# Three tiles of scans a batch instead of four, the fourth head pair joined by transfers, and state products in four tiles of TensorE

## The chip, the cores and the metric

One Trainium2 chip, one of its cores. TensorE (PE, with its weight loads PEld), VectorE (DVE), ScalarE (ACT) and GpSimd (POOL) each run their own list of instructions in order; SyncE (SP) issues nearly all DMA transfers. The metric is the device time of one execution in microseconds.

## The reference

A gated linear attention over 4 batches, 8 heads, 768 steps and head dimension 48, and on its output, for each batch, an MLP on the 128 rows (of 768) with the highest score:

```python
for t in range(S):
    state = alpha[:, :, t, :, None] * state + np.einsum('bhd,bhe->bhde', k[:, :, t], v[:, :, t])
    y[:, :, t] = np.einsum('bhd,bhde->bhe', q[:, :, t], state)
...
scores = np.einsum('bsd,d->bs', x, w_gate)
for b in range(B):
    top_idx = np.argpartition(-scores[b], capacity)[:capacity]
    xe = x[b, top_idx]
    h = np.maximum(xe @ w1, 0.0)
    ye = h @ w2
    g = 1.0 / (1.0 + np.exp(-scores[b, top_idx]))
    out[b, top_idx] = x[b, top_idx] + g[:, None] * ye
```

All inputs are fp32; x is y with the heads side by side (768 x 384), w1 is 384 x 1024, w2 1024 x 384.

## The kernel before

The work is cut into 16 head pairs: pair `i` is heads 2p and 2p+1 of batch `b`, with `i` = 4b + p. A pair's 2 x 48 rows (head dimension) lie in a tile of 128 partitions, head 0 in rows 0 to 47, head 1 in rows 64 to 111; rows 48 to 63 and 112 to 127 are padding. The 768 steps lie along the free dimension in 6 chunks of 128, with one extra column each (774 columns).

For each pair these steps run, under the names that the code and this text give them (the line numbers are of the kernel before):

- SP: `az` loads alpha, `kq` loads k and q, `v` loads v (the first three pairs in halves).
- DVE: `scan` (L314) makes running products of alpha from the end of each chunk into `su`, `end` (L321) their reciprocals, `fs` (L333) the running products from the chunk's start into `f`, `k` and `q` (both L343) multiply k into `su` and q into `f`. For the first three pairs these run in halves, and some of the half multiplies on POOL.
- ACT copies `gsu` (marks for a range check at the end) and, with POOL, `per` (the chunks' total decays).
- PE: `e` (L363) transposes the scaled keys, `a` (L375) makes the 128 x 128 products of keys and queries for each chunk, `d` (L398) the state that a chunk adds; ACT copies them out (`ev`, `me`, `u`), and POOL masks the products of `a` (`mk`, L392).
- DVE: `z` (L408) scans the states over the chunks. PE: `qz` (L416) multiplies queries by the state at the chunk's start, `av` (L424) adds the masked products times v; ACT copies the result into `x_sb` (`x`, L434).

`e`, `a`, `d`, `av` and `mk` come in two halves of three chunks, `.0` and `.1`. When a batch's four pairs are done, `out` stores it, DVE makes scores (`s`, L516, six a batch), PE and ACT spread them out along a row (`tp`, L545, and `tr`), ACT and DVE count for each row how many are greater (`c`, L562 and L569), DVE makes one-hots of the ranks (`oh`, L583), PE turns them into row indices (`f`, L590), DVE finishes those (`ix`), and POOL gathers the rows (`ga`, L612). Then comes the MLP: PE transposes the rows (`xt`, L626), multiplies by w1 (`h`, L650) and w2 (`y`, L663), DVE weights and adds (`ye`, L670), and POOL scatters (`sc`, L676). In names such as `f0` or `xt0` the number is the batch, in `qz2` or `e3.0` the pair.

The order on each engine isn't the order of the code. Every step is given to a planner (`Plan.order`) with an engine, a cost, the steps it needs, and a due number from the tables `DUE`, `SPOS`, `TPOS`, `MPOS` and others; the planner lists the steps by its own clock, and of the steps that could start at about the same time it takes the one with the lowest due number. Where it sees a gap on PE it places filler matmuls (L689) that multiply zeros. The lists are fixed when the program is built; on the chip each engine runs its list and waits where a step's inputs are missing. SP's list too is one queue: a transfer that waits for its source or its buffer holds all behind it.

`su` has three buffers, `f` four, `az` and `kq` two each, `vd` three.

Of the kernel before, what the change touches and what calls it, by code (L numbers as in the profile page):

```python
# [25 lines left out]
NI = B * NP  # L26
NV = 3
# [14 lines left out]
SPOS = (-18.633, -33.222, -6.621, 16.971)  # L42
TPOS = (5.402, 39.879, -70.789, 158.612)
CSTEP = 3.634
SSTEP = 2.177
DUE = {
    "az": -113.931, "kq": -28.063, "v": -80.603, "scan": 30.489, "end": -66.485, "gsu": -57.934, "fs": -37.912,
    "k": -61.696, "q": -32.659, "per": 123.388, "e": -165.343, "ev": 13.155, "a": -174.112, "me": -67.954,
    "mk": 6.777, "d": 60.08, "u": -49.58, "z": -85.3, "qz": 76.527, "av": 49.667, "x": -113.789, "out": 74.456,
}  # L50
DUE0 = {
    "az": 52.606, "kq": -31.386, "v": 132.261, "scan": 6.679, "end": 10.421, "gsu": -79.699, "fs": -9.968,
    "k": 123.63, "q": -23.229, "per": 77.238, "e": -129.958, "ev": -127.979, "a": -16.044, "me": 47.634,
    "mk": -113.768, "d": -21.156, "u": 80.088, "z": -49.321, "qz": -18.77, "av": -12.969, "x": 119.735,
    "out": -75.217,
}
DUE1 = {
    "az": -0.344, "kq": -51.834, "v": 76.44, "scan": -142.778, "end": -14.565, "gsu": 39.419, "fs": -102.264,
    "k": 98.732, "q": -74.419, "per": -37.278, "e": -16.987, "ev": 77.582, "a": 49.32, "me": 59.148, "mk": 30.542,
    "d": -40.158, "u": -0.174, "z": -86.612, "qz": 64.844, "av": -90.919, "x": -3.999, "out": 24.211,  # L60
}
DUEL = {
    "az": -91.202, "kq": -88.466, "v": -175.062, "scan": 61.758, "end": -66.725, "gsu": 120.319, "fs": 96.34,
    "k": 18.06, "q": -61.075, "per": -68.874, "e": -62.127, "ev": 20.986, "a": -31.455, "me": -24.017, "mk": 28.694,
    "d": 104.451, "u": -31.345, "z": 90.692, "qz": 61.069, "av": 113.285, "x": 7.473, "out": 15.166,
}
TUNE = ("SPOS", "TPOS", "CSTEP", "SSTEP", "MPOS", "MSTEP")
MPOS = (-40.121, 144.031, 188.924, -56.744)
MSTEP = (-17.234, 23.167, -4.221, 8.921)
HPIECE = (2, 2, 2, 2)  # L70
YPIECE = (2, 2, 2, 2)
NH = 3
MENG = "VG"
SCAN = (1.05, 1.75)
MULT = (0.55, 1.0)
ENDC = 0.22
ZC = 0.85
PENG = "AG"
# [102 lines left out]
def attention_topk_mlp(ctx: ExitStack, tc, cap, akq, vp, qn, kn, vn, an, wg, w1, w2, out):  # L181
# [27 lines left out]
    def fetch(i, to, at):  # L209
        nc.sync.dma_start(out=to, in_=akq[i // NP, i % NP, :, at])  # L210
# [99 lines left out]
    def prep_scan(i, r=slice(0, S)):  # L310
        az, w = loaded[i][0], span(r)
        if r.start == 0:
            scaled[i] = {"su": wk.tile([P, L], F32, name="su", bufs=3)}
# [677 lines left out]
```

## Time and profile before

| | us |
|---|---|
| three runs | 190.22, 191.06, 197.4 |
| median | 191.06 |
| the profiled execution | 189.88 |
| its span (first to last instruction) | 187.8 |

| engine | busy us in the span | share |
|---|---|---|
| PE | 171.3 | 91% |
| DVE | 146.5 | 78% |
| POOL | 110.1 | 59% |
| ACT | 94.2 | 50% |

Busy time of PE counts fillers as well as work, and each matmul's duration overlaps the next one's, so what a step costs PE is read from how far apart groups start, not from the duration of one. Transfers moved 33.71 MB.

### The profile page before, as it was taken

Reading aid. Unit: us, or ns where it says so; the run is one execution under the profiler, and the core shown is the slowest. Engines: PE = TensorE matmul, PEld = TensorE weight load, DVE = VectorE, ACT = ScalarE, POOL = GpSimd, SP = SyncE. Lnnn points to the kernel's source line nnn. Section 1 sums busy time; section 2 is a strip of 40 time slices with the busy share of each in tenths; the row PEclk is TensorE's granted clock in tenths of the full one; section 3 lists DMA queues with packets and bytes.
Section 4 is the critical chain, followed back from the end, with each engine's and each line's share of the span. In section 5 each row is a group of like instructions: output and inputs, shape, how many; then the busy total and the mean of one; then the engine's idle time right before and its main releaser. Section 6 shows DMA issues by size and latency. Waiting matters only on the chain.

```text
span 187.8 us, 5729 instructions
## 1 busy us (share of the span) xinstructions
PE 171.3 (91%) x2424; PEld 143.4 (76%) x2424; DVE 146.5 (78%) x239; ACT 94.2 (50%) x235; POOL 110.1 (59%) x101
## 2 busy tenths in 40 slices
PE   7989999999999979983999999999999999989930
PEld 2768878988898978872998689888889969759610
DVE  3999999999999999996649798899999946530010
ACT  4260763575468968551247956674648337111100
POOL 8399499999469919994029809639943400122020
PEclk9996999999999999998599999999999999999995
DMA  5996999993994269693520477637200061012010
GB/s 157 340 363 232 412 342 346 332 331 94 336 322 174 80 190 335 181 307 139 200 119 5 117 256 282 230 120 287 63 3 3 0 232 65 0 49 80 0 49 7
DMA packets 13903, 33.71 MB, mean 179 GB/s; under 512 B 1200, under 2 KB 7728, under 8 KB 13872
## 3 DMA queue, kind: packets, MB, share of 16 engines
q1 hardware_dynamic: 13360, 31.71, 49.6%
q0 software_dynamic: 512, 1.57, 2.5%
q8 instruction: 21, 0.34, 0.8%
q14 instruction: 10, 0.08, 0.1%
HBM read 27.77 MB, written 5.51 MB: 177 GB/s over the span
## 4 chain that ended last, share of the span: by engine, by line
PE 50%; DVE 9%; DMA 7%; POOL 6%; issue 2%; ACT 1%; DVEq 0%; POOLq 0%
PE MI L663 8%; PE MI L650 7%; DMA xe<-out,found 7%; PE PX L424 7%; PE PA L375 5%; POOL am L392 5%; PE PX L416 5%; DVE su L314 3%; PE KT L363 3%; PE PA L650 3%; PE PX L663 3%; PE PU L398 3%; DVE f L333 2%; PE KT L650 2%; PE PU L650 1%
## 5 line engine op out<-in xcount | busy, mean ns | idle before, releaser
L392 POOL TENSOR_SCALAR_AFFINE_SELECT am<-am 128x384 f32<-128x384 f32 x64 | 78.2, 1254 | 31.7 <-ACT am L388 31.7
L388 ACT COPY am<-PA 128x384 f32<-128x384 f32 x64 | 27.6, 485 | 14.5 <-PE PA L375 14.4
L314 DVE TENSOR_TENSOR_SCAN su<-az,dE 128x774 f32<-128x774 f32 (+1 forms) x19 | 32.5, 1721 | 2.2 <-DMA az<-akq 2.1
L333 DVE TENSOR_TENSOR_SCAN f<-az,d 128x774 f32<-128x774 f32 (+1 forms) x19 | 32.2, 1704 | 0.1
L375 PE MATMUL PA<-f,su 48*128 48x128 f32 x384 | 29.8, 287 | 1.3 <-DVE f L343 1.0
L424 PE MATMUL PX<-vd,am 128*64 128x48 f32 x768 | 29.1, 231 | 0.2 <-POOL am L392 0.2
L424 PEld LDWEIGHTS PX<-vd,am 128*64 128x64 f32 x768 | 25.9, 144 | 3.5 <-issue 1.0
L375 PEld LDWEIGHTS PA<-f,su 48*128 48x128 f32 x384 | 24.0, 187 | 3.8 <-DVE f L343 1.2
L416 PE MATMUL PX<-us,f 48*128 48x48 f32 x320 | 21.3, 290 | 0.8 <-DVE us L408 0.8
L416 PEld LDWEIGHTS PX<-us,f 48*128 48x128 f32 x320 | 19.1, 187 | 2.6 <-DVE us L408 1.3
L368 ACT COPY kt<-KT 128x336 f32<-128x336 f32 x32 | 14.3, 445 | 10.5 <-PE KT L363 10.4
L408 DVE TENSOR_TENSOR_SCAN us<-us,per 112x287 f32<-112x287 f32 x16 | 14.4, 906 | 4.9 <-ACT us L404 4.7
L516 DVE SCALAR_TENSOR_TENSOR junk<-x_sb,wgb 128x384 f32<-128x384 f32 (+2 forms) x30 | 16.4, 589 | 1.1 <-ACT x_sb L434 1.1
L363 PE MATMUL KT<-ident,su 112*128 112x112 f32 x96 | 16.1, 277 | 0.5 <-DVE d L321 0.3
L663 PE MATMUL MI<-w2s,hh 128*128 128x384 f32 x48 | 16.5, 490 | 0.0
L562 ACT ACTIVATE sgn<-row,sc 128x768 bf16<-128x768 f32 x17 | 16.0, 939 | 0.3
L434 ACT COPY x_sb<-PX 128x288 f32<-128x288 f32 x32 | 11.2, 401 | 9.6 <-PE PX L424 9.4
L343 DVE TENSOR_TENSOR f<-kq,f 128x768 f32<-128x768 f32 (+1 forms) x16 | 15.8, 1004 | 0.0
L612 POOL DMA_INDIRECT xe<-out,found x4 | 5.7, 1415 | 17.0 <-DVE fk L708 13.6
L343 DVE TENSOR_TENSOR su<-kq,su 128x768 f32<-128x768 f32 (+1 forms) x16 | 15.5, 978 | 0.0
L676 POOL DMA_INDIRECT out<-ye,found x4 | 4.3, 1083 | 18.0 <-DVE ye L670 8.9
L689 PEld LDWEIGHTS <-warm 128*128 128x128 bf16 x143 | 13.2, 99 | 1.5 <-issue 0.3
(96 smaller groups left out, 228.0 us busy)
## 6 DMA issues: line engine op xcount, KB each, us to landing
kq<-akq SPq DMA_DIRECT2D x13, 768.0 KB, 6.2
az<-akq SPq DMA_DIRECT2D x13, 387.0 KB, 3.5
vd<-vp SPq DMA_DIRECT2D x16, 288.0 KB, 3.4
out<-x_sb SPq DMA_DIRECT2D x4, 1152.0 KB, 5.5
kq<-akq SPq DMA_DIRECT2D x12, 192.0 KB, 4.9
w2s<-w SPq DMA_DIRECT2D x1, 1536.0 KB, 10.0
w1s<-w SPq DMA_DIRECT2D x1, 1536.0 KB, 10.9
az<-akq SPq DMA_DIRECT2D x6, 193.5 KB, 4.3
```

The lines of the kernel that those rows point to most:

```text
L314: V.tensor_tensor_scan(out=scaled[i]["su"][:, w][:, ::-1], data0=az[:, w][:, ::-1], data1=dE[:, w][:, ::-1], initial=0.0, op0=ALU.mult, op ...
L333: V.tensor_tensor_scan(out=scaled[i]["f"][:, w], data0=az[:, w], data1=d1[:, w], initial=0.0, op0=ALU.mult, op1=ALU.add,)
L343: (G if e == "G" else V).tensor_tensor(out=to[:, c], in0=by.rearrange("p (c t) -> p c t", t=C)[:, c], in1=to[:, c], op=ALU.mult,)
L363: T.transpose(out=KT[:, j * R:(j + 1) * R], in_=keys(i)[0:R, 3 * g + j], identity=ident[0:R, 0:R])
L375: T.matmul(out=bank_a(i, c // 3, h)[:, (c % 3) * C:(c % 3 + 1) * C], lhsT=keys(i)[own(h), c], rhs=queries(i)[own(h), c], start=True, stop= ...
L388: A.copy(out=ams[i][:, h, g * HS:(g + 1) * HS], in_=bank_a(i, g, h)[:, 0:HS])
L392: G.affine_select(out=part, in_=part, compare_op=ALU.is_ge, fill=0.0, base=0, pattern=[[0, 3], [1, C]], channel_multiplier=-1,)
L416: T.matmul(out=PX[h][:, c * D:(c + 1) * D], lhsT=queries(i)[own(h), c], rhs=uss[i][own(h), :, c - 1], start=c == 1, stop=False, skip_group ...
L424: T.matmul(out=PX[h][m:m + ROW, c * D:(c + 1) * D], lhsT=ams[i][:, h, c * C + m:c * C + m + ROW], rhs=vrows(i, h, c), start=False, stop=Tr ...
L516: V.scalar_tensor_tensor(out=junks[blk % 2][:, cols], in0=xs[b][:, blk, cols], scalar=1.0, in1=wgb[:, cols], op0=ALU.mult, op1=ALU.mult, a ...
L650: T.matmul(out=self.banks[1 + g][:, ff * P:(ff + 1) * P], lhsT=w1s[:, cc, fi * P:(fi + 1) * P], rhs=self.xet[:, cc * P:(cc + 1) * P], star ...
L663: T.matmul(out=self.banks[3][:, 0:E], lhsT=self.hh[:, fi * P:(fi + 1) * P], rhs=w2s[:, fi, :], start=(fi == 0), stop=(fi == F // P - 1),)
```

## The change

**Three tiles a batch.** Rows 48 to 63 and 112 to 127 of each tile no longer hold padding. The fourth pair of a batch (p = 3) is cut into three pieces of 16 rows for each of its heads, and each piece rides in the spare rows of one of the other three tiles, from the input on (`layout`). DVE scans and multiplies 12 tiles `u` (three a batch) instead of 16 pairs, so that `scan`, `end`, `fs`, `k` and `q` now count tiles: tile `u` = 3b + p serves pair 4b + p. For the fourth pair, transfers from SBUF to SBUF (`spread`, L327 of the changed kernel) copy the 16 spare rows of each head of the finished `su` (steps `sk`) and `f` (steps `sq`) into tiles `join0` and `join1`, on which `e`, `a`, `per` and `qz` of that pair then work. That is two transfers for each of 24 steps, on SP's queue. A fourth pair needs the transfers of all three tiles. The first two tiles run in halves (before, the first three pairs), all multiplies are on DVE, all `per` copies on ACT.

**State products in four tiles of TensorE.** `qz` (L438) was one matmul for each chunk and head, with 48 rows and 128 columns of weights; it becomes two with 64 columns each, the upper and the lower half of the output.

**The planner's numbers.** All due tables are new, some costs too, so the order of the steps is new on every engine.

The core of the diff, the tables cut to a line:

```diff
+NT = NP - 1
+NU = NT * B
+NSU, NF = 3, 4
-SPOS = (-18.633, -33.222, -6.621, 16.971)
+SPOS = (0.481, 6.575, 32.031, -5.558)
...
-NH = 3
+NH = 2
...
-PENG = "AG"
+SPREAD = 1.0
+PENG = "A"
...
+    joined = [[const.tile([P, L], F32, name=f"join{g}_{j}") for j in range(2)] for g in range(2)]
+    for j in range(2):
+        for rows in (slice(32, 64), slice(96, 128)):
+            G.memset(joined[0][j][rows], 0.0)
...
+    def heads(i, g):
+        b, p = divmod(i, NP)
+        return unit(NT * b + p, g) if p < NT else joined[g][b % 2]
+
+    def spread(u, g):
+        b, n = divmod(u, NT)
+        for h in range(2):
+            at = h * ROW + n * (ROW - D)
+            nc.sync.dma_start(out=joined[g][b % 2][at:at + ROW - D], in_=unit(u, g)[h * ROW + D:(h + 1) * ROW])
...
     def pe_qz(i, c):
         for h in range(2):
-            T.matmul(
-                out=PX[h][:, c * D:(c + 1) * D], lhsT=queries(i)[own(h), c],
-                rhs=uss[i][own(h), :, c - 1], start=c == 1, stop=False, skip_group_check=True,
-            )
+            for m in range(0, C, ROW):
+                T.matmul(
+                    out=PX[h][m:m + ROW, c * D:(c + 1) * D], lhsT=queries(i)[own(h), c, m:m + ROW],
+                    rhs=uss[i][own(h), :, c - 1], start=c == 1, stop=False, skip_group_check=True,
+                )
...
+        for g, (nm, src, old) in enumerate((
+            ("sk", "k", [f"a{i}.1", f"e{i}.1", f"per{i}"]), ("sq", "q", [f"a{i}.1", f"qz{i}"]),
+        )):
+            add(f"{nm}{u}", "D", SPREAD, lambda u=u, g=g: spread(u, g), [f"{src}{u}", f"{src}{u}.0", f"{src}{u}.1"] + old, at(i, nm), late=0.9)
...
-            f"qz{i}", "P", 1.22, lambda i=i: [pe_qz(i, c) for c in range(1, NC)],
+            f"qz{i}", "P", 0.70, lambda i=i: [pe_qz(i, c) for c in range(1, NC)],
```

Three places show how the order moved. The first is DVE's list around batch 0's one-hots (`oh`), whose second half releases `f0`. Before, the one-hots stand among the scans and multiplies (`su`, `f`) of the pairs 7, 8 and 9:

```order
L343 TENSOR_TENSOR f_980<-kq_1_80,f_980 128x6x128
L343 TENSOR_TENSOR f_1001<-kq_0_79,f_1001 128x6x128
L583 TENSOR_TENSOR oh_1040<-slotrow_116,rk_943 128x384
L314 SCALAR_TENSOR_TENSOR su_1054<-az_1_78,dE_93 128x774
L408 SCALAR_TENSOR_TENSOR us_1072<-us_1072,per_1_103 112x287
L321 RECIPROCAL d1_1_102<-su_1054 128x6
L583 TENSOR_TENSOR oh_1040<-slotrow_116,rk_943 128x384
L333 SCALAR_TENSOR_TENSOR f_1112<-az_1_78,d1_1_102 128x774
```

Now they stand among those of tile 6, the first of batch 2, with three of the counts (`cnt`) ahead of them:

```order
L337 SCALAR_TENSOR_TENSOR su_0_130<-az_0_77,dE_93 128x774
L591 SCALAR_TENSOR_TENSOR cnt_147,rk_901<-row_853,sc_800,ones_f_118 128x768 x2
L344 RECIPROCAL d1_0_100<-su_0_130 128x6
L591 SCALAR_TENSOR_TENSOR cnt_147,rk_901<-row_853,sc_800,ones_f_118 128x768
L354 SCALAR_TENSOR_TENSOR f_2_135<-az_0_77,d1_0_100 128x774
L601 TENSOR_SCALAR rk_901<-rk_901 128x3
L605 TENSOR_TENSOR oh_1023<-slotrow_116,rk_901 128x384
L364 TENSOR_TENSOR f_2_135<-kq_0_79,f_2_135 128x6x128
L605 TENSOR_TENSOR oh_1023<-slotrow_116,rk_901 128x384
L429 SCALAR_TENSOR_TENSOR us_1037<-us_1037,per_0_101 112x287
L620 TENSOR_SCALAR bad_1082<-KT_73 128x1
```

Ahead of the second one-hot stand the scans of seven tiles instead of ten pairs, and behind it, ahead of the index (`bad`), one `z` (`us`).

The second is PE's list around `f0` (`oh` as weights), each line of dots leaving out rows that repeat the ones above. Before, `f0` stands behind `a8.1` and ahead of `av7`:

```order
L416 MATMUL PX0_70<-us_1072,f_980 128x48
L416 MATMUL PX1_71<-us_1072,f_980 128x48
...
L375 MATMUL PA1_68<-f_1001,su_916 128x128
L375 MATMUL PA2_69<-f_1001,su_916 128x128
...
L590 LDWEIGHTS oh_1040
L590 MATMUL KT_73<-place_117,oh_1040 128x3
...
L424 MATMUL PX0_70<-vd_1_82,am_1049 64x48 x2
L424 MATMUL PX1_71<-vd_1_82,am_1049 64x48 x2
```

Now it stands behind `d7.1`, and behind it come the second half of `a7` (a fourth pair, on `join`), and `qz6`, whose matmuls are pairs of 64 columns:

```order
L419 MATMUL PU_72<-vd_1_82,kt_929 48x48 x12
L612 LDWEIGHTS oh_1023
L612 MATMUL KT_73<-place_117,oh_1023 128x3
...
L396 MATMUL PA0_67<-join1_1_140,join0_1_138 128x128
L396 MATMUL PA1_68<-join1_1_140,join0_1_138 128x128
...
L438 MATMUL PX0_70<-us_1037,f_1_134 64x48 x2
L438 MATMUL PX1_71<-us_1037,f_1_134 64x48 x2
...
L446 MATMUL PX0_70<-vd_0_81,am_988 64x48 x2
```

`f0` has moved ahead by about a pair and a half of attention work.

The third is SP's list where the weights of the MLP are loaded. Before, loads alone:

```order
L297 DMA wgb_127<-wg 128x384
L294 DMA w2s_129<-w2 128x8x384
L210 DMA az_1_78<-akq 128x774
L229 DMA vd_0_81<-vp 128x576
L210 DMA kq_1_80<-akq 128x1536
L210 DMA az_0_77<-akq 128x774
```

Now the transfers into `join` stand between them (`join0` from `su`, `join1` from `f`):

```order
L327 DMA join0_0_137<-su_1_131 16x774 x2
L304 DMA wgb_127<-wg 128x384
L217 DMA kq_1_80<-akq 128x1536
L301 DMA w2s_129<-w2 128x8x384
L327 DMA join0_0_137<-su_2_132 16x774 x2
L217 DMA az_0_77<-akq 128x774
L327 DMA join1_0_139<-f_2_135 16x774 x2
L236 DMA vd_0_81<-vp 128x576
```

Each of them waits on SP until DVE has finished the tile it reads.

## Rows read from the trace of the kernel before

**Rows 1.** The page, busy us, share and instructions of each engine
```profile
PE 171.3 (91%) x2424; PEld 143.4 (76%) x2424; DVE 146.5 (78%) x239; ACT 94.2 (50%) x235; POOL 110.1 (59%) x101
```

**Rows 2.** Windows: stretch and length, busy of five engines, PEclk, DMA share, GB/s
```profile
8.00:75.40 67.40, 65.00 (x1091) 56.52 (x1092) 66.99 (x82) 41.03 (x105) 55.53 (x41) 0.97 0.81 279
75.40:87.80 12.40, 8.30 (x163) 7.11 (x161) 10.56 (x17) 5.40 (x14) 11.18 (x10) 0.98 0.75 234
87.80:125.10 37.30, 37.19 (x523) 31.55 (x523) 30.36 (x40) 22.36 (x57) 17.64 (x13) 0.91 0.47 158
...
179.72:187.80 8.08, 0.19 (x2) 0.09 (x2) 0.77 (x2) 0.00 (x0) 0.98 (x1) 0.70 0.11 32
```

**Rows 3.** Groups of DVE by form: busy us, mean ns of one | idle before
```profile
L333 DVE TENSOR_TENSOR_SCAN f<-az,d 128x774 f32<-128x774 f32 x13 | 25.6, 1971 | 0.1
L314 DVE TENSOR_TENSOR_SCAN su<-az,dE 128x774 f32<-128x774 f32 x13 | 24.9, 1918 | 0.2 <-PE PA L375 0.2
L408 DVE TENSOR_TENSOR_SCAN us<-us,per 112x287 f32<-112x287 f32 x16 | 14.4, 906 | 4.9 <-ACT us L404 4.7
L343 DVE TENSOR_TENSOR su<-kq,su 128x768 f32<-128x768 f32 x13 | 13.9, 1076 | 0.0
...
L314 DVE TENSOR_TENSOR_SCAN su<-az,dE 128x387 f32<-128x387 f32 x6 | 7.6, 1296 | 2.1 <-DMA az<-akq 2.1
L569 DVE SCALAR_TENSOR_TENSOR cnt<-row,sc,ones_f 128x768 bf16<-128x768 f32 x7 | 7.5, 1073 | 3.3 <-ACT row L553 3.1
L333 DVE TENSOR_TENSOR_SCAN f<-az,d 128x387 f32<-128x387 f32 x6 | 6.7, 1123 | 0.0
...
L343 DVE TENSOR_TENSOR f<-kq,f 128x384 f32<-128x384 f32 x3 | 2.5, 840 | 0.0
```

**Rows 4.** Timeline of DVE: start us, us, instruction (first scan, second one-hot)
```profile
3.42 0.96 DVE L314 TENSOR_TENSOR_SCAN su<-az,dE 128x387 f32<-128x387 f32 x1 [1.72 <-DMA az<-akq]
...
72.78 0.72 DVE L583 TENSOR_TENSOR oh<-slotrow,rk 128x384 bf16<-128x384 f32 x1
```

**Rows 5.** Chain that ended last: start us, us to the next piece, records
```profile
81.31 6.45 DMA xe<-out,found
...
96.84 1.53 PE MI L650 x12
98.38 0.87 PE PA L375 x12
...
107.43 1.27 PE PX L416 x20
108.70 0.83 PE PX L424 x24
...
111.67 0.44 PE KT L363 x3
112.11 0.68 PE PU L398 x24
...
153.69 0.33 PE KT L545 x3
...
162.57 0.13 PE KT L590 x6
...
174.54 5.18 PE MI L663 x16
```

**Rows 6.** Timeline of PE: batch 0's top-k step, and its first MLP step
```profile
75.37 0.30 PE L590 MATMUL KT<-place,oh 128*128 128x3 bf16 x6
...
87.80 0.90 PE L626 MATMUL MI<-ident,xe 128*128 128x128 f32 x3 [3.81 <-DMA xe<-out,found]
```

**Rows 7.** The page's costliest group on POOL, the masks
```profile
L392 POOL TENSOR_SCALAR_AFFINE_SELECT am<-am 128x384 f32<-128x384 f32 x64 | 78.2, 1254 | 31.7 <-ACT am L388 31.7
```

**Rows 8.** DMA issues: size of one, median us to landing
```profile
vd<-vp SPq DMA_DIRECT2D x16, 288.0 KB, 3.4
...
w1s<-w SPq DMA_DIRECT2D x1, 1536.0 KB, 10.9
```

## What the change should do to the time

> **What bounds the kernel now.** I read the shares of the engines first [rows 1]: PE is busy 91% of the span and DVE 78%, which as averages over stages with different limits decide nothing. So I cut the span where the chain of waits changes its character, and read busy time by stage [rows 2]. From 8 to 75.4 us DVE is busy 66.99 of 67.4 us: it never stops, and it is what sets the end of that stage. [...] At 75.37 comes `f0` (L590), PE's step in batch 0's top-k, released by the last one-hot on DVE, which ends at 73.50 [rows 4, 6]. From then on the roles change: in the stage from 87.8 to 125.1 PE is busy 37.19 of 37.3 us, and DVE 30.36. [...] Behind PE's last matmul the span runs another 8.08 us (weighted sum, scatter, end) [rows 2].
>
> So the time is: `f0`, set by DVE, plus PE's list from `f0` to its last matmul, plus what PE stands still in that list, plus 8.08, plus 2.08 (the profiled execution is 189.88, its span 187.8). I check this on the kernel before. From `f0` on PE issues 14 `a` steps at 0.87, 18 `av` at 0.83, 14 `e` at 0.44, 15 `d` (two in 0.68), 8 `qz` at 1.27, 16 `h` at 1.53, four times the eight `y` matmuls at 5.18, 4 `f` at 0.13, and 10 `tp` or `xt` at 0.33 [rows 5]: 97.6 us. The wall from 75.37 to 179.72 is 104.35. The remainder is 6.75, of which 3.81 is the stop and 2.9 the slower clock behind it, eight fillers and small waits.
>
> **Term 1: DVE up to `f0`.** In the order of the changed kernel, DVE has finished tile 6 where it had begun tile 10. Counted on both orders from the first scan (3.42) to the second one-hot of batch 0 (before: 73.50): half scans 6 to 4 in each direction, full `scan` 7 to 5, full `fs` 6 to 5, full multiplies 12 to 9, half multiplies 6 to 8 (POOL's six are gone), `z` 8 to 6, and three counts (`c0`) that ACT made before. With [rows 3]: -2 x 1.30 - 2 x 1.12 - 2 x 1.92 - 1.97 - 3 x 1.08 + 2 x 0.84 - 2 x 0.91 + 3 x 1.07 = -10.8. The one-hot ends at 62.7, and `f0`, for which PE then waits, starts at 63.0. PE is not late there: with the same prices its real work ahead of `f0` is about 41 us, of the 55 from its first step at 8 us.
>
> **Term 2: PE from `f0` on.** More stands behind `f0` than before, since DVE reaches it with fewer pairs done: 17 `a` (14.8), 20 `av` (16.6), 16 `e` (7.0), 16 `d` (5.4), and the same h, y, f, tp and xt (24.5, 20.7, 0.5, 3.3): 92.8 us without `qz`, of which there are 10.
>
> What a `qz` costs in four tiles no row of before shows. Today it is 20 records in 1.27, 63.5 ns apart; the change makes them 40, with half the weight columns. The upper bound is `av`, whose weights also have 64 columns and which uses two column tiles: 24 records in 0.83, 34.6 ns apart; 40 of these are 1.38, more than today. The lower bound: splitting rows takes a record with 128 weight and 128 moving columns from 127 ns (`h`, 12 in 1.53) to 72 ns (`a`, 12 in 0.87), a factor of 0.57; `av`'s spacing times that is 20 ns, 0.79. The closest spacing of any two records in this trace is `f`'s, 6 in 0.13, or 21.7 ns [rows 5]. I take that one, since it is nearest to what both splits together give: 40 x 21.7 = 0.87, so 10 x 0.87 = 8.7. The table in the diff books 0.70; taken as an outer end, it is 1.7 less over ten. The six `qz` ahead of `f0` gain nothing, since PE has room there.
>
> [...]
>
> The list is then 101.5 us and would end at 164.5.
>
> **Term 3: what PE stands still.** Between `f0` and `xt0` PE now has 2 `a`, 2 `qz`, 3 `av`, 2 `e` and a `d`: 7.3 us with `f` [rows 5], so it is at `xt0` at 70.3. The index is ready about 1.3 us after `f0` (a `z`, 0.91 [rows 3], stands ahead of it on DVE); from the gather's issue to `xt0` it took 6.45 [rows 5]. If POOL is free the rows are there at 70.8, a wait of 0.5. Before, POOL had a queue of masks ahead of the gather; now one mask of pair 7 (`mk7.0.0`) stands directly before it, and the other three behind it. Two masks late, at 1.25 each [rows 7], would make the wait 3.0. I take 1.0. The remainder of 2.9 I keep whole. The later gathers have more cover: 10 us of PE's work from `f1` to `xt1`, 8 from `f2` to `xt2`, 5.4 from `f3` to `xt3`, as before.
>
> **What costs nothing, and its cover.** The 48 transfers of the spare rows (two for each of 24 steps) go out on SP. A fourth pair can start only when the keys of all three tiles have landed. For pair 3: between `k2` and `e3.0` DVE makes `q2`, `scan3`, `z1`, `end3`, `fs3` and `z2`, and PE `qz2`: 1.08 + 1.92 + 0.91 + 0.2 + 1.97 + 0.91 + 0.87 = 7.8 us of cover [rows 3]. The landing of such a transfer is not in the trace; the shortest median there is 3.4 us (288 KB) and the longest 10.9 (1536 KB) [rows 8]. With some 0.9 for the issue of two, everything up to 6.9 is covered. These move 48 KB each, so I take the near end, and nothing is added. SP stands behind each of them until DVE has the product; `az` and `kq` of later tiles, and at the end `v14` and `out2`, queue with them. The loads have a tile's time of lead (6 us of scans and multiplies), so the first few us of such a delay are covered too. Without POOL's multiplies (six) and copies (five), POOL has less to do; ACT gets those five copies and is half idle.
>
> **Sum.** 63.0 + 101.5 + 1.0 + 2.9 = 168.4 for PE's last matmul; + 8.08 + 2.08 = 178.5. The profiled execution stood 1.2 under the median of the three runs (191.06) and 0.3 under the fastest; I add 0.5 for that: **179.0**.
>
> **Rivals.** (a) *The four tiles don't overlap.* `qz` goes at `av`'s spacing, 1.38; ten times 0.51 more: 184.1. For it: `av` and `d` have two tiles, and their spacing (34.6 and 28 ns) still follows their weight columns (64 and 48), as if one load ran at a time. Against it: rows split in two brought `a` to 0.57 of `h`. [...]
>
> (b) *DVE gives its gain back before `f0`.* It waits for a load or for a `us` copy, where before it stood 0.4 us in 67. Each us that `f0` is late is a us at the end, since PE's list behind it stays as long. At `f0` = 70 the time is 186.0; with all 10.8 lost, 189.8. Against it: fewer bytes are loaded for the same pairs.
>
> (c) *The transfers land late, and the kernel becomes slower.* All come from SP and share the queue with loads and w1, w2. If each of the four joined pairs had pair 3's cover, they would decide against the change from a landing of 9.9 us (4 x 3.0 takes the 12 us won). At the longest landing in the trace, 10.9, each pair is 4.0 late: 195.0, slower than before.
>
> **Chances.** Forecast 0.52, (a) 0.15, (b) 0.21, (c) 0.12. The bounds of the forecast: `qz` at 0.70 (-1.7), no wait at `xt0` (-1.0), no remainder (-2.9) give 173.4; the wait at 3.0 and `qz` at 1.0 give 182.3. The range reaches on through (a) and most of (b): 173.0 to 188.0, which leaves out (c) and the last of (b). About 2% is what a measurement of this kernel can tell from no change: faster means under 187.2. Forecast, (a) and half of (b) are there: 0.78. The other half of (b) and a part of (c) lie within 2%: 0.14. The rest of (c), 0.08, is slower.
>
> **What would show it.** `f0` (L612 in the changed kernel) at 63 +- 2; later than 67 says (b), and DVE's idle time ahead of it names the cause. `qz` (L438): 40 records in 0.7 to 1.0 from the chain, against 1.38 for (a). `xt0` (L648) at 71 to 73, with PE idle before it under 3 us, and no granted clock near 0.9 in the stage behind. Landing of `join` under 7 us, and no wait for it in front of L384 or L396. PE's last matmul at 168. If it is late although `f0` and `qz` are as said, the sum over PE's list has failed: PE would then show idle time behind `f0`, and what ended it (a mask, a `z`, a `join`) is the step I have missed.

## The result, and the profile after

The changed kernel takes 177.71 us (median; 175.85 to 181.26), the kernel before 190.64 on the same chip: a ratio of 0.930, with a 95% interval of 0.920 to 0.941. The forecast was 179.0. The profile that came with these runs belongs to an execution of 181.26 us with a lower granted clock (0.962; 0.988 to 0.991 in the other three), so the kernel was profiled once more (E0 below, 177.99 us, span 176.1), and its rows are read here.

The page's line of engines and the windows answer to [rows 1, 2]; stages are cut at `f0`, at `xt0`, where DVE's share falls (125 us) and behind PE's last matmul:

```profile
PE 163.5 (93%) x2727; PEld 135.0 (77%) x2727; DVE 124.2 (71%) x232; ACT 91.9 (52%) x225; POOL 78.0 (44%) x94
```

The windows:

```profile
8.00:66.14 58.14, 55.52 (x1061) 47.24 (x1062) 51.14 (x78) 34.84 (x88) 30.18 (x30) 0.97 0.88 288
66.14:73.94 7.80, 7.80 (x205) 6.79 (x201) 7.42 (x11) 5.25 (x14) 7.25 (x5) 1.00 0.54 184
73.94:125.00 51.06, 51.06 (x973) 43.11 (x969) 43.47 (x71) 33.66 (x84) 24.06 (x28) 1.00 0.57 180
125.00:168.74 43.74, 43.17 (x473) 34.66 (x469) 17.59 (x67) 15.69 (x37) 8.49 (x12) 1.00 0.14 46
168.74:176.10 7.36, 0.19 (x2) 0.09 (x2) 0.77 (x2) 0.00 (x0) 1.00 (x1) 0.68 0.10 35
```

DVE has 22 us less work, and from `f0` to its last matmul PE is busy 102.03 of 102.60 us (7.80 + 51.06 + 43.17) at a granted clock of 1.00. Ahead of `f0` the roles have changed: DVE is busy only 51.14 of 58.14 us, where it had 66.99 of 67.40 [rows 2].

DVE's groups by form, against [rows 3]:

```profile
L354 DVE TENSOR_TENSOR_SCAN f<-az,d 128x774 f32<-128x774 f32 x10 | 18.0, 1796 | 0.1
L337 DVE TENSOR_TENSOR_SCAN su<-az,dE 128x774 f32<-128x774 f32 x10 | 17.7, 1783 | 1.7 <-DMA az<-akq 1.7
L429 DVE TENSOR_TENSOR_SCAN us<-us,per 112x287 f32<-112x287 f32 x16 | 14.7, 923 | 9.5 <-ACT us L425 9.5
...
L337 DVE TENSOR_TENSOR_SCAN su<-az,dE 128x387 f32<-128x387 f32 x4 | 4.0, 1027 | 2.7 <-DMA az<-akq 2.7
```

The second one-hot in DVE's timeline, against [rows 4]:

```profile
62.70 0.87 DVE L605 TENSOR_TENSOR oh<-slotrow,rk 128x384 bf16<-128x384 f32 x1
```

Not only are there fewer scans, each is shorter (1783 ns where it was 1918, a half scan 1027 where it was 1296). Over the whole span `z` waits 9.5 us for ACT's copy of the state, which comes from PE (before 4.7); only 1.4 of it lie ahead of the second one-hot.

PE's timeline at four places (the third and fourth answer to [rows 6]):

```profile
34.64 0.35 PE L384 MATMUL KT<-ident,join 112*128 112x112 f32 x2 [1.07 <-issue]
48.12 0.20 PE L419 MATMUL PU<-vd,kt 128*48 128x48 f32 x1 [0.75 <-issue]
66.14 0.31 PE L612 MATMUL KT<-place,oh 128*128 128x3 bf16 x6
...
73.94 0.55 PE L648 MATMUL MI<-ident,xe 128*128 128x128 f32 x3
```

Pieces of the chain that ended last, against [rows 5]:

```profile
21.40 1.02 PE PX L438 x40
22.42 1.53 PE PX L446 x48
...
28.59 1.01 PE PX L438 x40
```

`f0` starts 2.57 us after the one-hot has ended (62.70 + 0.87), so PE itself is late. `xt0` finds its rows there. A `qz` takes 1.02 us. Twice ahead of `f0` PE stands (1.07 and 0.75 us), and the profile knows no engine that it waits for ("issue").

The masks, a quarter shorter than in [rows 7]:

```profile
L413 POOL TENSOR_SCALAR_AFFINE_SELECT am<-am 128x384 f32<-128x384 f32 x64 | 59.1, 947 | 60.1 <-ACT am L409 60.0
```

The transfers into `join`: KB of one, median us to landing, against [rows 8]:

```profile
join<-su SPq DMA_DIRECT2D x24, 48.4 KB, 4.1
```

### The profile page after: what moved, and what is told of

The parts are those of the page before. It is cut to its first block, busy times and chain, and to the rows that moved or that the text cites. A ratio compares the mean times of both kernels' runs of the same rounds, so it can differ in the third digit from the quotient of the medians.

```text
span 179.5 us, 6378 instructions
## 1 busy us (share of the span) xinstructions
PE 166.9 (93%) x2727; PEld 137.2 (76%) x2727; DVE 124.0 (69%) x232; ACT 92.1 (51%) x225; POOL 78.5 (44%) x94
## 4 chain that ended last, share of the span: by engine, by line
PE 80%; issue 6%; DVE 6%; DMA 2%; SPq 1%; ACT 1%; POOL 1%; DVEq 0%
PE PA L396 15%; PE PX L446 14%; PE PX L438 9%; PE KT L384 7%; PE MI L672 7%; PE MI L685 6%; PE PU L419 6%; PE PA L672 3%; PE PX L685 3%; DMA az<-akq 2%; PE PX L711 2%; PE PU L711 2%; PE KT L567 2%; PE KT L672 2%; PE PU L672 1%
## 5 line engine op out<-in xcount | busy, mean ns | idle before, releaser
L413 POOL TENSOR_SCALAR_AFFINE_SELECT am<-am 128x384 f32<-128x384 f32 x64 | 59.6, 954 | 62.5 <-ACT am L409 62.3
L337 DVE TENSOR_TENSOR_SCAN su<-az,dE 128x774 f32<-128x774 f32 (+1 forms) x14 | 21.8, 1566 | 4.7 <-DMA az<-akq 4.7
L396 PE MATMUL PA<-f,su 48*128 48x128 f32 x288 | 23.2, 295 | 0.0
L429 DVE TENSOR_TENSOR_SCAN us<-us,per 112x287 f32<-112x287 f32 x16 | 14.8, 932 | 10.8 <-ACT us L425 10.8
L354 DVE TENSOR_TENSOR_SCAN f<-az,d 128x774 f32<-128x774 f32 (+1 forms) x14 | 21.9, 1562 | 0.1
L396 PEld LDWEIGHTS PA<-f,su 48*128 48x128 f32 x288 | 18.6, 192 | 2.9 <-issue 0.7
L538 DVE SCALAR_TENSOR_TENSOR junk<-x_sb,wgb 128x384 f32<-128x384 f32 (+2 forms) x30 | 15.4, 564 | 4.7 <-ACT x_sb L456 4.7
L591 DVE SCALAR_TENSOR_TENSOR cnt<-row,sc,ones_f 128x768 bf16<-128x768 f32 x12 | 12.2, 1016 | 3.7 <-ACT row L575 3.5
L419 PE MATMUL PU<-vd,kt 128*48 128x48 f32 x384 | 14.6, 217 | 0.0
L419 PEld LDWEIGHTS PU<-vd,kt 128*48 128x48 f32 x384 | 11.3, 128 | 3.6 <-issue 0.9
L438 PE MATMUL PX<-us,f 48*64 48x48 f32 x480 | 13.1, 265 | 0.2 <-DVE us L429 0.2
L384 PE MATMUL KT<-ident,su 112*128 112x112 f32 x72 | 12.4, 283 | 0.7 <-DVE su L364 0.7
```

Source lines behind the costliest of these rows:

```text
L337: V.tensor_tensor_scan(out=unit(i, 0)[:, w][:, ::-1], data0=az[:, w][:, ::-1], data1=dE[:, w][:, ::-1], initial=0.0, op0=ALU.mult, op1=ALU ...
L354: V.tensor_tensor_scan(out=unit(i, 1)[:, w], data0=az[:, w], data1=d1[:, w], initial=0.0, op0=ALU.mult, op1=ALU.add,)
L384: T.transpose(out=KT[:, j * R:(j + 1) * R], in_=keys(i)[0:R, 3 * g + j], identity=ident[0:R, 0:R])
L396: T.matmul(out=bank_a(i, c // 3, h)[:, (c % 3) * C:(c % 3 + 1) * C], lhsT=keys(i)[own(h), c], rhs=queries(i)[own(h), c], start=True, stop= ...
L413: G.affine_select(out=part, in_=part, compare_op=ALU.is_ge, fill=0.0, base=0, pattern=[[0, 3], [1, C]], channel_multiplier=-1,)
L419: T.matmul(out=PU[own(h), c * D:(c + 1) * D], lhsT=kts[i][:, c, own(h)], rhs=vrows(i, h, c), start=True, stop=True,)
```

## The experiments

**E0: the changed kernel, unaltered.**

> The changed kernel once more, unaltered, for a second profile. In its first profile PE stood 2.04 us in the middle of e3.0 (32.31 to 34.35), the granted clock then sat at about half in slices from 32 to 46 us, and f0 came at 69.0 instead of the forecast 63.0. Theory A (that stop and the slower clock behind it are an accident of the one execution): the second profile has f0 at 63 to 66, a span of 174 to 176 and no stop of 2 us in e3.0. Theory B (they belong to the kernel): f0 is at 68 to 70 again, behind a stop at the same place. In both, qz (L438) goes at 40 records in 1.02 us from chain to chain, and PE's list from f0 to the last matmul takes 102 to 103 us.

Measured 179.39 us (177.99 to 182.76), ratio 0.946 (0.938 to 0.953). Its rows stand above. Both profiles of this kernel have the stop in `e3.0` (2.04 us in the first, 1.07 here); in the first the granted clock behind it was 0.50 from 38 to 46 us, and `f0` came at 69.00. One kernel, the same stop, and `f0` at 66 or at 69: much of what follows is about that stop.

**E1: only the four tiles of `qz` undone.**

```diff
-            for m in range(0, C, ROW):
-                T.matmul(out=PX[h][m:m + ROW, c * D:(c + 1) * D], lhsT=queries(i)[own(h), c, m:m + ROW], ...)
+            T.matmul(out=PX[h][:, c * D:(c + 1) * D], lhsT=queries(i)[own(h), c], ...)
```

> The changed kernel with qz as before, one matmul of 128 weight columns for a chunk and head; the order of the steps on every engine is unaltered. Theory (only the ten qz behind f0 count, the six ahead of it lie in PE's spare time): 10 x (1.27 - 1.02) = 2.5 us longer than the changed kernel, 179.5 to 180.5. Rival (all sixteen count, as PE has no spare time ahead of f0 either): 16 x 0.25 = 4.0 us longer. Rival (the halved weights change nothing on PE, since what bounds it is elsewhere): within 0.5 us of the changed kernel.

Measured 178.43 (177.91 to 178.6), ratio 0.943 (0.938 to 0.947). So nearly the whole gain stands without the four tiles. DVE's last one-hot ahead of `f0`, and PE's `f0`, `xt0` and last group of `y`:

```profile
60.07 0.87 DVE L604 TENSOR_TENSOR oh<-slotrow,rk 128x384 bf16<-128x384 f32 x1
...
63.76 0.31 PE L611 MATMUL KT<-place,oh 128*128 128x3 bf16 x6
...
71.86 0.55 PE L647 MATMUL MI<-ident,xe 128*128 128x128 f32 x3
...
162.89 5.33 PE L684 MATMUL MI<-w2s,hh 128*128 128x384 f32 x16
```

No stop is left on PE from 20 us up to `f0`, and the one-hot ends at 60.94, 2.6 us earlier than in E0, `f0` starts 2.4 earlier. The list behind `f0` is 104.46 us (162.89 + 5.33 - 63.76), that of E0 102.60: there the four tiles win 1.9 us.

Not all of the 2.4 us ahead of `f0` is theirs. The first `qz` is already 1.7 us later in E0, though up to there both kernels have the same list:

```profile
8.74 0.48 PE L384 MATMUL KT<-ident,su 112*128 112x112 f32 x3 [1.69 <-POOL xe L628]
...
21.33 1.09 PE L438 MATMUL PX<-us,f 48*64 48x48 f32 x40
```

The same place in E1:

```profile
19.64 1.34 PE L437 MATMUL PX<-us,f 48*128 48x48 f32 x20 [0.23 <-DVE us L429]
```

In E0's execution the second load of alpha came 0.8 us later, PE stood 1.69 us, and its granted clock from 8 us to the first `qz` was 0.87 (1.00 in E1). From there E0 falls behind at its two stops by 2.2 us and regains 0.25 at each of six `qz`. So the four tiles ahead of `f0` cost a net 0.7 us in this execution; counted the same way, from the first `qz` to `f0` and against E1, it is 1.1 in E10 below and 4.9 in the first profile, where the clock fell to 0.50.

**E2: only the four tiles, in the kernel before.** The same edit, forwards, in the old order.

> The kernel before with only the four-tile qz, in its old order. Theory: of its 16 qz, 8 stand behind f0, where PE has work without a gap; 8 x 0.25 = 2.0 us less than before, about 1%. What is left of the change (three tiles, joining transfers, new order) is then worth some 10 of the 12 to 13 us. Rival (the packing is the larger part): 4 us or more less. Rival (PE stands as long for the gathers as it saves): no change.

Measured 189.01, ratio 0.997 (0.992 to 1.003): no change. PE waits longer, for the gathered rows 4.3 us instead of 3.81 [rows 6], and for DVE's keys:

```profile
PE MI L627 <- DMA xe<-out,found: 4.3, 1, 4.3
PE KT L363 <- DVE su L343: 2.2, 2, 1.7
```

In this profile the list behind `f0` is still 1.9 us shorter (102.43, before 104.33) and `f0` 0.6 later; in the ratio nothing of that is left.

**E5: four tiles only behind `f0`.**

```diff
+        w = ROW if i >= 6 else C
-            for m in range(0, C, ROW):
+            for m in range(0, C, w):
```

> The changed kernel with qz in four tiles only from pair 6 on (the ten behind f0), and whole, as before, for pairs 0 to 5. Theory F (the packing shortens PE's list behind f0 by 2.5 us, and loses the same ahead of f0, where its extra instructions make PE run out of fetched instructions and stand at a boundary of 256 of them): no stop of PE in e3.0, f0 at 63 to 64, list behind f0 102 us, so 175.5 to 176.5, 2 to 2.5 us less than with all qz whole. Rival (the packing has no worth, and the shorter list behind f0 is eaten by other waits): 178 as with all qz whole.

Measured 175.96 (175.39 to 176.38), ratio 0.926 (0.921 to 0.932): 2.5 us faster than E1, and faster than the changed kernel. PE has no stop without a releaser, and its granted clock is 1.00 from 8 us to its last matmul:

```profile
63.56 0.31 PE L613 MATMUL KT<-place,oh 128*128 128x3 bf16 x6
...
71.36 0.55 PE L649 MATMUL MI<-ident,xe 128*128 128x128 f32 x3
...
160.83 5.33 PE L686 MATMUL MI<-w2s,hh 128*128 128x384 f32 x16
```

The list behind `f0` is 102.60 us, as in E0. So the ten `qz` behind `f0` give 1.9 us by the list and 2.5 by the medians, and the six ahead of it cost more than they give.

**E10: what the stop hangs on.** 32 one-column matmuls at PE's start (64 more instructions), nothing else.

```diff
+    for n in range(32):
+        spin(1, PU)
```

> The changed kernel with 32 matmuls of one column ahead of the first step, 64 more instructions at a place where PE waits anyway. Theory F (PE stands where a block of 256 instructions ends that is not there yet): the stop of 1 to 2 us leaves e3.0 and, if it comes, comes at the 961st matmul or weight load again, which is now 64 instructions earlier in the program, inside qz2. Rival (e3.0 waits for a transfer into join): the stop stays in e3.0, behind its first transpose.

Measured 177.88 (one execution). The stop has left `e3.0` and stands inside `qz2`, as expected, and a smaller one has appeared in an `a` step:

```profile
27.10 0.71 PE L396 MATMUL PA<-f,su 48*128 48x128 f32 x6 [0.33 <-issue]
...
33.85 0.90 PE L438 MATMUL PX<-us,f 48*64 48x48 f32 x30 [1.44 <-issue]
```

So it is tied to a place in PE's list of instructions, not to a step. Counting all of PE's records (matmuls, weight loads and the few of its sequencer) from the start of each trace up to a gap of over 0.5 us that no engine explains:

```
kernel                   records begun   gap starts   start to start
changed, first profile        961           32.05          2.31 us
E0                            961           33.31          1.33
E0                           1473           47.16          0.95
E10                           705           26.50          0.60
E10                           961           32.14          1.71
E6 (below)                   4033          115.30          1.36
```

The numbers differ by multiples of 256, and 961 comes back in different kernels. The page has a queue of its own for instructions:

```profile
q8 instruction: 23, 0.38, 0.8%
```

0.38 MB in 23 packets is 16.5 KB each; in the trace of the first profile each has 16,384 bytes. There, taken in order, the first twenty go with PE's records 449, 705, 961 and so on to 5313, each ahead of its record but that of 961; that a packet brings the next 256 is my reading of this. The packet of record 961 ran from 31.93 to 33.04, while PE reached that place at 32.05 and went on at 34.35. In E0 such a packet ran from 32.31 to 33.42 while PE reached record 961, and PE went on at 34.64; in E1 the packet of that place began at 30.69, when PE was still at record 793, and nothing stood. In all traces of this case PE passes 267 such places. It stands there without a releaser at the six of the table alone: those that it reaches before their packet has ended or within 0.9 us after, and it goes on 1.2 to 1.5 us after that end. At every other place it arrives 1.2 us or more after the end, and passes. A late packet costs 0.3 to 2.0 us of idle time here, and behind the one of 2.04 us, in the first profile, the granted clock was 0.50 from 38 to 46 us.

Four tiles double the instructions of a `qz` (80 in 1.02 us instead of 40 in 1.27), so PE arrives at the next such place sooner. Why the packet comes late just there isn't settled: the 1536 KB load of w2 is under way at that time, which E3 tried to show, and so are the transfers into `join`. Without these (E9) the packet of record 961 begins 0.3 us before PE passes record 705, the place before it; in E5 it begins 3.1 us behind that.

**E3: w2's load moved behind `kq4` on SP.**

```diff
+    late = next(s for s in steps if s[2] == "w2")
+    steps.remove(late)
+    steps.insert(1 + next(n for n, s in enumerate(steps) if s[2] == "kq4"), late)
```

> The changed kernel with the load of w2 (1536 KB) moved on SP's list behind kq4, five transfers later, so that sk2, az4, sq2, az5 and kq4 no longer stand behind it. Theory (w2's bytes ahead of the transfers of tile 2 make e3 late, and the clock pays for that): 1 to 4 us less than the changed kernel, with no stop of PE at e3. Rival (the stop is not of the transfers' making): the same time within 1 us, and the stop, if it comes, at the same instruction.

Measured 184.03 as median over a wide spread (one execution at 176.29, five from 182.64 to 185.56); the profiled one took 184.49. The stop in `e3.0` is gone, but `v4` now queues behind w2 on SP, and PE stands for it at 42 us; behind that its granted clock reads 5 or 6 tenths in five slices. The wait:

```profile
PE PU L419 <- DMA vd<-vp: 2.0, 1, 2.0
```

The clock in 40 slices:

```profile
PEclk9999999996555699999999999999999999999995
```

One stop was exchanged for another; what w2 does to the instruction queue stays open.

**E6: E5 without the 25 fillers between `tp0.0` and `f0`.**

```diff
+    seen = [s[2] for s in steps]
+    first, last = seen.index("tp0.0"), seen.index("f0")
+    steps = [s for n, s in enumerate(steps) if s[2] != "fill" or not first < n < last]
```

> As e5_late_four, and without the 25 filler matmuls that stand on PE's list between tp0.0 and f0. Theory (ahead of f0 it is PE's own list, fillers included, that is late: in the run with whole qz DVE's one-hot ended 2.8 us before f0 and PE had not stood still since 20 us): f0 2 to 2.8 us earlier, at 61 to 61.7, and the end as much earlier, 173.5. Rival (DVE sets f0, as forecast): f0 and the end unchanged within 0.5 us. Rival (the fillers carry the clock): the granted clock drops to its lower level behind f0 and the time grows by 2 us or more.

Measured 177.56 as median over a wide spread (174.37 to 189.85); the profiled execution has a span of 173.2, E5's 173.7. The one-hot and `f0`:

```profile
60.02 0.55 DVE L606 TENSOR_TENSOR oh<-slotrow,rk 128x384 bf16<-128x384 f32 x1
...
62.09 0.30 PE L613 MATMUL KT<-place,oh 128*128 128x3 bf16 x6
```

The one-hot ends at 60.57 (61.20 in E5), and `f0` is 1.47 us earlier than in E5: the fillers had delayed it. But the list behind it is 104.0 us, 1.4 longer than E5's, since another stop without a releaser has come:

```profile
116.66 0.29 PE L419 MATMUL PU<-vd,kt 128*48 128x48 f32 x4 [1.16 <-issue]
```

It stands at record 4033, twelve times 256 behind 961, and the packet of that place ran from 114.27 to 115.15: it is of the same kind as the others. Of the 1.5 us the profile's end shows 0.1. Fillers delay `f0`, yet taking them out wins nothing certain.

**E8: the saved work put back on DVE.** E5, with dummy scans and multiplies of a fourth tile's size once a batch; the result is unaffected.

```diff
+    def fourth():
+        ...  # two scans of 128x774 and two multiplies of 128x768, into a spare tile
...
+            if ready[u] == 2 and u % NT == NT - 1:
+                fourth()
```

> As e5_late_four, with the scans and multiplies of a fourth tile put back on DVE for each batch (two full scans and two full multiplies on a spare tile, about 5.7 us, behind the products of tiles 2, 5, 8 and 11; nothing reads them). Theory (the time that DVE saves ahead of f0 is the gain): two of the four stand ahead of f0, 11.4 us, of which DVE's idle time (3.3 us) and its lead over f0 (2.8 us) absorb up to 6; f0 at 69 to 72 and the time 182 to 185. Rival (the new order of the steps is the gain, DVE has room): f0 within 2 us of e5_late_four and the time under 179.

Measured 198.07 (197.49 to 198.72), ratio 1.044: 22 us slower than E5, for 24.2 us more DVE time, and slower than before. I had expected 182 to 185. PE's waits:

```profile
PE PX L439 <- DVE us L429: 7.1, 5, 4.1
PE KT L568 <- DVE junk L539: 2.3, 3, 1.4
```

Its granted clock in 40 slices:

```profile
PEclk9999996699997569999999999995799999999995
```

`f0` comes at 78.20 (14.6 later than in E5, for two lots of dummy work ahead of it, 11 us), and the list behind it is 110.2 us instead of 102.6. The rest of the price lies in stops ahead of and behind `f0` and in the lower clock behind the longer of them (0.66 from 30 to 40 us, 0.57 from 60 to 70). In this order, which was not made for it, a us of DVE's work costs nearly a us of the kernel, and not only ahead of `f0`; an order that knew of the dummy work might pay less.

**E7 and E11: the order alone.** The kernel before with the changed kernel's due tables. In E7 it was not given the changed kernel's rule that a load into `kq` waits for the `k` multiply too, so some `k` multiplies read the keys of a later pair; E11 adds the rule.

```diff
-            add(f"kq{i}", "D", 2.05, ..., [f"az{i}", f"q{i - 2}", f"q{i - 2}.1"], ...)
+            add(f"kq{i}", "D", 2.05, ..., [f"az{i}", f"q{i - 2}", f"q{i - 2}.1", f"k{i - 2}", f"k{i - 2}.1"], ...)
```

> The kernel before, 16 pairs of tiles and whole qz, with the changed kernel's due numbers (all four tables, the places of scores, top-k and MLP) and nothing else. In its order DVE has, up to the second one-hot of batch 0, three full scan and two fs fewer than the kernel before, four multiplies and a z fewer, and three counts more: 11.7 us less, so f0 comes at about 64 in this kernel too, but with nine pairs of DVE work left behind it instead of six tiles less. Theory (what is gained is DVE's work, and the order only uses it): PE finds fewer finished pairs behind f0, waits there for su, f or us at several places, and the clock falls behind those stops: 186 to 194 us, no better than the 189 to 191 of before. Rival (the order is the gain, any kernel with f0 at 64 and pairs kept behind it would have it): PE runs on behind f0 without stops, 177 to 182 us, as E1 with 178.4.

> E7 again, with the one rule that it lacked: a load into a kq buffer now also needs the k multiply of the pair that used it (the changed kernel has this rule; the kernel before has only the q multiply, and in the new order k comes after q, so in E7 a load overtook it, the multiply read the keys of a later pair, and DVE waited 3.8 us for loads there). 16 pairs of tiles, whole qz, the changed kernel's due numbers. Theory (DVE's saved work is the gain; the order only uses it): the waits of E7 in the stretches 8 to 30 and 60 to 100 us shrink, but DVE still has nine pairs behind f0 and PE runs out of finished pairs: 186 to 198 us. Rival (the order is the gain, and E7 was only spoilt by its loads): 177 to 183 us.

E7 took 205.95 us, E11 195.0 (194.16 to 196.6), ratio 1.026 (1.017 to 1.035): slower than before. In E11's timeline, `f0` and the last group of `y`:

```profile
64.40 0.30 PE L593 MATMUL KT<-place,oh 128*128 128x3 bf16 x6
...
180.75 5.33 PE L666 MATMUL MI<-w2s,hh 128*128 128x384 f32 x16
```

Its fillers behind `f0`, from the groups of that stretch:

```profile
L692 PE MATMUL PX<-warm 128*128 128x224 bf16 x81 | 10.0, 272 | 0.0
L692 PE MATMUL PU<-warm 128*128 128x224 bf16 x25 | 2.9, 259 | 0.0
```

`f0` is nearly as early as in E1 and E5 (63.76 and 63.56), and nothing is gained: the list behind it is 121.7 us, 17.2 more than E1's with the same `qz`. The planner, which knows that DVE still has nine pairs to do, fills PE's gaps with 106 fillers (12.9 us busy; E1 has none behind `f0`). An early `f0` alone is worth nothing here; the work behind it must be ready.

**E9: E5 without the transfers.** The `join` tiles hold zeros, and the fourth pairs wait for no transfer.

```diff
     def spread(u, g):
...
-        for h in range(2):
...
-            nc.sync.dma_start(out=joined[g][b % 2][at:at + ROW - D], in_=unit(u, g)[h * ROW + D:(h + 1) * ROW])
+        pass
```

> This is E5 (whole qz up to pair 5, four tiles from pair 6) with the 48 transfers into the join tiles left out; the join tiles hold zeros instead, so the fourth pair's heads are wrong, and the fourth pairs wait for none of the transfers. Everything else, the orders of all engines and SP's loads too, stays. Theory (the transfers are covered: their median landing was 3.8 to 4.0 us against 7.8 us of cover, and nothing on PE or DVE waited for join): within 1 us of E5's 175.96, f0 within 0.5 us of 63.6, xt0 within 0.5 of 71.4. Rival (they cost something that no wait shows, by holding SP's list or by sharing the DMA engines with the loads that DVE reads): 2 to 4 us faster than E5, so 172 to 174, with f0 before 62.5 or the list behind it shorter than 103.

Measured 176.16 (175.78 to 176.34), ratio 0.934 (0.931 to 0.937), no faster than E5. In E5 the 48 transfers cost nothing.

**E12: E5 with the `q` multiplies of the first two tiles on POOL.**

```diff
-add(f"q{u}{w}", "V", m, lambda e="V", u=u, r=r: prep_q(u, e, r), ...)
+add(f"q{u}{w}", "V", m, lambda e="G" if u < NH else "V", u=u, r=r: prep_q(u, e, r), ...)
```

> E5 with one change: the four half multiplies of q into f (tiles 0 and 1) run on POOL, as some did in the kernel before, with every list's order kept. DVE's work up to batch 0's one-hots shrinks by four times 0.54 = 2.2 us. In the kernel before and in E11, where POOL has six such multiplies, DVE's half scans took 1.18 to 1.30 us for su and 1.12 to 1.33 for f, against 1.03 and 1.05 in the changed kernel. Theory (a POOL multiply beside them is what lengthens DVE's scans and multiplies, so taking POOL's multiplies away gave DVE about 5 us that the prediction did not count): the half scans go back to 1.1 to 1.3 us on the mean, some of the masks ahead of 1.2 us appear, POOL's multiply takes 1.3 to 1.8 us, and nothing is won: 176 to 179 us. Rival (the prices fell for another reason, such as the tiles' spare rows or fewer loads): half scans stay within 0.03 us of 1.03 and 1.05, and DVE is up to 2 us earlier at the one-hots.

Measured 182.92 (two runs), ratio 0.966 (0.946 to 0.986): 7 us slower than E5, more than expected. DVE's timeline in E12, where POOL multiplies, among others, from 7.50 to 8.74 and from 14.99 to 17.77:

```profile
4.60 0.96 DVE L354 TENSOR_TENSOR_SCAN f<-az,d 128x387 f32<-128x387 f32 x1
...
7.89 1.67 DVE L354 TENSOR_TENSOR_SCAN f<-az,d 128x387 f32<-128x387 f32 x1
...
15.76 1.20 DVE L364 TENSOR_TENSOR su<-kq,su 128x384 f32<-128x384 f32 x1
16.88 2.52 DVE L337 TENSOR_TENSOR_SCAN su<-az,dE 128x774 f32<-128x774 f32 x1
```

The same four instructions in E5, with POOL idle of multiplies:

```profile
4.66 0.96 DVE L354 TENSOR_TENSOR_SCAN f<-az,d 128x387 f32<-128x387 f32 x1
...
7.77 0.95 DVE L354 TENSOR_TENSOR_SCAN f<-az,d 128x387 f32<-128x387 f32 x1
...
15.54 0.55 DVE L364 TENSOR_TENSOR su<-kq,su 128x384 f32<-128x384 f32 x1
16.01 1.76 DVE L337 TENSOR_TENSOR_SCAN su<-az,dE 128x774 f32<-128x774 f32 x1
```

DVE's busy time is 125.2 us (E5: 124.5), although multiplies of 2.2 us have left it. With a multiply on POOL beside them a half scan took 0.72 us longer, a half multiply 0.65, a full scan 0.76. Over the kernel half scans have a mean of 1.21 and 1.23 us here, 1.02 and 1.05 in E5: the theory holds, and the rival falls. POOL's multiplies take from DVE what they do for it. Of the 7 us, 1.9 stand at `f0` (65.43); the other 5.6 come behind it, where PE stands 2.39 us at `xt0`; the granted clock of the execution is 0.967, E5's 0.987.

## Why the prediction came out, step by step

The end was right, the path to it only in part: `f0` came 3.1 us late, the list behind it took 2.8 less than its parts had been given, and that the two nearly cancel is luck. Beside the prediction's sum stand E0's times (us):

| | predicted | E0 |
|---|---|---|
| second one-hot ends | 62.7 | 63.57 |
| `f0` starts | 63.0 | 66.14 |
| list from `f0`, remainder included | 101.5 + 2.9 | 102.60 |
| wait at `xt0` | 1.0 | 0 |
| PE's last matmul ends | 168.4 | 168.74 |
| behind it, and outside the span | 8.08 + 2.08 | 7.36 + 1.89 |
| the execution | 178.5 | 177.99 |

**Term 1, DVE's work: right in direction, mis-sized twice.** From the first scan to the one-hot's end DVE is busy 53.84 us, where it was 69.20 of 70.08: 15.4 less, not 10.8. The counts were right, the prices [rows 3] too high. With the prices of after, five full scans and five `fs` are 0.14 and 0.18 us cheaper, four halves of each 0.27 and 0.07, and the half multiplies add 0.5 us (eight in 4.5, six before in 4.1) instead of 1.7: together 4.1 more. For the halves the cause is POOL's multiplies, which lengthen what runs beside them (E12: a half scan by 0.72 us, a half multiply by 0.65). For the full scans it isn't: the last of POOL's six multiplies before ended at 23.94, and the first full scan began at 24.28. There the trace points to POOL's other work, masks and `per` copies. Two scans of the kernel before, the first with two masks beside it, the second with nothing of POOL:

```profile
38.63 2.08 DVE L314 TENSOR_TENSOR_SCAN su<-az,dE 128x774 f32<-128x774 f32 x1
...
109.45 1.76 DVE L314 TENSOR_TENSOR_SCAN su<-az,dE 128x774 f32<-128x774 f32 x1
```

Of its 26 full scans 16 took over 1.9 us, each with masks or `per` copies beside it; after, 2 of 20 did. But some scans with masks beside took no longer than 1.77, and no run changed the masks alone, so this cause is not shown. On the other side DVE is idle 6.4 us there, where it was 0.9: 2.7 for loads of alpha, 1.9 for what ACT makes of the scores, 1.4 for ACT's copies of states. In E1, without PE's stops, it is idle 3.3 us, and the one-hot ends at 60.94.

**"PE is not late there": the step that failed.** The real work ahead of `f0` was put at 41 us of the 55 and the rest taken as slack. The work was right: of E0's 58.14 us PE is busy 55.52, and 13.8 of these are 107 fillers, which leaves 41.7. (Before, the stage had 114 fillers, 13.8 us.) But the fillers stand in the fixed list and do not yield to anything. The list is full, and PE, not DVE, sets `f0`: 2.8 us after the one-hot in E1, 2.6 in E0, 1.5 in E6, where 25 fillers are out. I counted the fillers of the old kernel as a cover and forgot that a cover in an in-order list is work. For the same reason "the six `qz` ahead of `f0` gain nothing" failed both ways: with no room on PE each gains its 0.25 us, and the stops at places a multiple of 256 records apart, which no row of before had shown, take more than that, 2.2 us in E0. The other 1.7 us of E0's delay against E1 are that execution's late start.

**Term 2, the list behind `f0`: right, with its price for `qz` too low.** `qz` takes 1.02 us (40 records, 25.5 ns apart on the mean), not 0.87. The 21.7 ns behind that price were a misreading: the chain's 0.13 us run from the end of the step before to the end of `f`, while `f`'s six records start over 0.15 us, 25 to 26 ns apart but for the first pair:

```profile
162.41 0.29 PE L590 MATMUL KT<-place,oh 128*128 128x3 bf16 x6
162.56 0.69 PE L650 MATMUL PU<-xet,w1s 128*128 128x128 f32 x4
```

`f`'s spacing does not explain that of `qz`: in E0 its records start in fours, most of them 6 to 10 ns apart, with some 60 to 80 ns to the next four (before, in twos 6 ns apart, with 105 to the next), and only the mean comes near 25. No run shows the 1.0 that the forecast's upper bound takes for a `qz`; E0's chain shows 1.02. With 1.02 the list is 92.8 + 10.2 = 103.0, measured 102.60; with 1.27, for E1, 105.5, measured 104.46.

**Term 3: too careful.** There is no wait at `xt0`: from `f0` to `xt0` PE works 7.80 us (predicted 7.3), and the rows are there. Before, PE stood 3.81 us there [rows 6], and the granted clock behind that was 0.50 from 87.8 to 93 us and 0.80 from 93 to 96. With the stop went the slower clock behind it, so the remainder of 2.9 went too: the stage from `xt0` on has a granted clock of 1.00, where the old one had 0.91 [rows 2]. These 3.9 us pay for the 3.1 by which `f0` came late.

**The transfers: right.** They land in 4.1 us in the median (the longest took 9.1 in E0), PE waits for none (DVE once, 1.1 us in E1 and 0.8 in E5), and leaving them out of E5 changes nothing (E9: 176.16 against 175.96). The 0.9 booked for the issue of two is what two loads of alpha took on SP before (0.91, at 4.10); two into `join` took 1.1 to 1.2 in the first profile (medians of one 0.54 from `su`, 0.58 from `f`). **The tail: 0.7 us short**, by 7.36 instead of 8.08.

**The rivals.** (a) fell: 1.02 is not 1.38, and the records of four tiles start within some 25 ns, so they do overlap. (b) had the place right, and the cause mostly wrong: `f0` came at 66 and at 69 in the two profiles, and DVE did wait 2.7 us for loads in E0, but the one-hot was done 2.6 us before `f0`, which PE's list and its stops held. (c) fell with E9.

**Where the gain comes from.** Of the three parts, neither the four tiles alone (E2, 0.997) nor the new due numbers alone (E11, 1.026) give anything; three tiles with whole `qz` give 0.943 (E1), and with DVE's work put back nothing is left (E8). It is the work taken from DVE together with an order made for it; no run has three tiles in the old order. Part of that work is that POOL no longer multiplies beside DVE's instructions (E12). What stays open: what delays the instruction packets (w2's load, the transfers into `join`, or all transfers together), and why the full scans are shorter.

## What to carry to other kernels

In a fixed, in-order list, count fillers as work: when the engine that feeds the list gets faster, they can become the bound (E6: 25 fewer, `f0` 1.47 us earlier, though the end gained nothing certain). Splitting a matmul into more, shorter ones paid here behind `f0`, where PE is the bound and its instructions arrive in time (1.9 us of the list, E5), and ahead of it cost a net 0.7 us (E0): find the places in the list where the engine stands without a releaser, and split elsewhere, as E5 does. Before moving work from DVE to POOL, look at what DVE's instructions take while POOL runs (a half scan 1.67 us instead of 0.95, E12).

## What the hardware showed that I had not expected

- PE stood 0.3 to 2.0 us at fixed places of its instruction list, a multiple of 256 records apart, when an instruction packet (16,384 bytes) came late, and went on 1.2 to 1.5 us after the packet's end; 64 instructions more at the start moved the stop from one step to another (E10).
- Beside a multiply on POOL a DVE scan took up to 1.8 times as long (1.67 against 0.95 us, E12); the 16 full scans of the kernel before that took over 1.9 us all had other work of POOL beside them.
- Behind stops of PE of 2 to 4 us there are stretches of a lower granted clock (E3 2.0 us, 5 or 6 tenths in five slices; E8 4.1, 0.66 over 10 us; the first profile of the changed kernel 2.0, 0.50 over 8 us; the kernel before 3.81, 0.50 over 5 us); E0's stop of 1.07 has none (the mean up to `f0` is 0.97, and the 0.87 up to the first `qz` accounts for it).
